# Clustered attention, mixture of experts and gated MLP on one core: mask copies, idle-time matmuls and expert 0's input moved

## The chip, the cores and the metric

The program runs on one core of a Trainium2 chip. The metric is device microseconds of one execution, and before the change it is 753.95 us (median of three runs, 753.9 to 755.81). TensorE (PE) multiplies and writes PSUM; VectorE (DVE) and ScalarE (ACT) read PSUM; GpSimd (POOL) works on SBUF; SyncE (SP) issues nearly all DMAs. Each engine runs its instructions in program order and waits on semaphores.

## The reference

Three stages follow each other (shapes in brackets).

```python
# attention: q, k, v [2, 8, 768, 64], 16 centroids per head
mask = argmax(q_n @ c_n)[:, :, :, None] == argmax(k_n @ c_n)[:, :, None, :]
scores = where(mask, q @ k.T / 8, -1e9)
attn = exp(scores - max) / (sum + 1e-9)
x = (attn @ v)                                   # -> [1536, 512]
# mixture of experts: each token to one of 8, at most 384 tokens each
e = argmax(x @ w_gate);  p = softmax(x @ w_gate)[e]
x = p * (relu(x @ w1[e]) @ w2[e])                # w1 [8, 512, 1024]
# gated MLP
out = (silu(x @ w_gate2) * (x @ w_val)) @ w_out  # 512 -> 1536 -> 512
```

## The kernel before

**Attention.** The 16 heads (2 batches of 8) are worked on as 8 pairs; an even and an odd head share a pair. A head has 6 query tiles of 128, so there are 96 tiles, and one loop (`run`, L504) goes over them. In the loop's step for tile g stand, in the order of `CFG['order']`: the exponentials of tile g+1 (`soft`, ACT, L378, out P), the sums of a finished group of three tiles (`evac`), the scores of tile g+2 (`qk`, four PE products, L365, out s, followed by a DVE maximum, L368, out nm), the transposes of tile g's P (`pt`, PE L397; one half copied by ACT, L400, the other by DVE, L402), then a list of extra steps for that tile (`bg[g]`: the first at B0, the others at B1), and every third tile the product with v (`pv`, L416, out acc). Score tiles have two PSUM buffers, so `qk` of tile g+2 waits until `soft` has read tile g.

**Preparation of a pair.** A pair's q and k are loaded (`load`, ldq, ldk), transposed by PE (`tr`, L169), split by ACT, DVE and POOL into a rounded part H and a rest L, and moved by DMAs (`moves`, L150) into the operands Aq, Ak, qB, kB. The cluster masks join the score product as 16 extra rows of qB and kB: `assign`, `pick`, `first` make a one-hot matrix, and `mask` writes its transpose to a tile oT (ACT) and moves it into qB and kB by four small DMAs. `CFG['offs']` and, for pair 1, `CFG['offs1']` say in which tile each step is issued, counted from the start of the pair before; pair 2's k is transposed first in tile 9 (offset -3 before tile 12). Pair 0 is prepared ahead of the loop: `mask0` (L277) writes the even head's rows straight into qB and kB, then copies all four row groups to oT (DVE the q rows, L305; ACT the k rows, L306) and moves the odd head's rows by two DMAs. The odd head of pair 0 starts at tile 6.

**SP's queue.** DMAs are issued in program order. With the code before, after pair 0's moves come: the two mask moves from oT, six small loads of the gate weights (`unit`, R and R2), the six q moves of pair 1, the loads of pair 2's q and k (four DMAs of 192 KB, issued in tile 0), the six k moves of pair 1 (192 KB each), and pair 1's four mask moves.

**The clock filler.** `warm` (L498) issues n transposes of the identity whose result nobody reads.

**Expert 0 during the last tiles.** Weight blocks of 128x1024 come through a pool of four buffers named raw (`load`, L947). Expert 0's eight blocks are split by quarters (`piece(i, k, eng)`, L972): half k of block i is rounded by ACT (eng 1) or POOL (eng 0), L982, and POOL takes the rest, L983. After the second half of a block the step named in L986 follows, such as the next load. `head` (L989) loads 128 token rows xa into a raw buffer; `slots` takes another raw buffer XA, into which `take_head` (L1007) writes their transpose split in two. Pieces run from the loop's extra steps (`spare`, L1541) and around `evac` (`pieces`, L1540). `tail` (L1066) finishes expert 0's first 128 tokens (`head1` by W1, `fold`, `head2` by W2) while the last tokens are scattered to their experts' rows. Experts and gated MLP follow and are untouched.

Of the kernel before, what the change touches and what calls it, by code (L numbers as in the profile page):

```python
# [10 lines left out]
F32 = mybir.dt.float32  # L11
F32R = mybir.dt.float32r
# [11 lines left out]
class Attention:  # L24
# [137 lines left out]
    def tr(self, n, nm, half):  # L162
# [10 lines left out]
        nc.scalar.activation(out=Ht[:, sl], in_=flat, func=AF.Copy, scale=s)  # L173
        if CFG["xe"]["qk".index(nm)] == "a":
            nc.scalar.activation(out=X[:, sl], in_=flat, func=AF.Copy, scale=s)  # L175
# [102 lines left out]
    def mask0(self):  # L278

        nc, st = self.nc, self.pairs[0]  # L280
        J, C, S = self.J, self.C, self.S
        HJ = J // 2
        st["oT"] = self.one.tile([4 * C, S], F32R, tag="oT", name="oT")
        ohv = st["oh"].rearrange("p j s c -> p j (s c)")
        ps = []
        for half in range(2):
            t = self.ps_m.tile([4 * C, HJ, 128], F32, tag="mm", name="otp")
            for jj in range(HJ):
                nc.tensor.transpose(t[:, jj, :], ohv[:, half * HJ + jj, :], self.ident)
            ps.append((slice(half * HJ * 128, (half + 1) * HJ * 128), t.rearrange("p j t -> p (j t)")))  # L290
        q, k = slice(0, 2 * C), slice(2 * C, 4 * C)

        def queries(sl, flat):
            nc.vector.tensor_copy(st["Bq"][64:64 + C, 0, sl], flat[0:C])

        def keys(sl, flat):
            nc.scalar.activation(out=st["Bk"][64:64 + C, 0, sl], in_=flat[2 * C:3 * C], func=AF.Identity,
                                 scale=self.sc[2 * C:3 * C, 0:1], bias=self.sc[2 * C:3 * C, 1:2])

        keys(*ps[0])  # L300
        queries(*ps[1])
        keys(*ps[1])
        queries(*ps[0])
        for sl, flat in ps:
            nc.vector.tensor_copy(st["oT"][q, sl], flat[q])  # L305
            nc.scalar.activation(out=st["oT"][k, sl], in_=flat[k], func=AF.Identity, scale=self.sc[k, 0:1],  # L306
                                 bias=self.sc[k, 1:2])
        for si, nm in enumerate("qk"):
            r0 = 2 * si * C
            self.move(st["B" + nm][64 - C:64, 1], st["oT"][r0 + C:r0 + 2 * C])  # L310

    def mask(self, n, half):
        nc, st = self.nc, self.pairs[n]
# [189 lines left out]
    def run(self, cent, gate, early, fill, after, spare, pieces, go):  # L503
# [5 lines left out]
        bg = {}  # L509
        for n in range(1, self.NP):  # L510
            s0 = 2 * J * (n - 1)
            st = self.prep_steps(n)
            for nm, o in CFG["offs" if n > 1 else "offs1"]:
                if n == 1 and nm in ("q0", "q1"):
                    continue
                bg.setdefault(s0 + o, []).append(st[nm])
            if n + 1 < self.NP:
                bg.setdefault(s0 + CFG["load"], []).append(lambda n=n: self.load(n + 1, "qk"))
            if n > 1:
                bg.setdefault(s0 + 5, []).append(lambda n=n: self.load(n, "v"))  # L520
        self.warm(self.ps_m, "mm", 13)
# [11 lines left out]
        a = [self.assign0(0), self.assign0(1)]  # L533
# [1 line left out]
            next(a[i])  # L535
        low = self.tr0(1, "q")
        self.warm(self.ps_m, "mm", 18)
        self.mask0()
        self.unit(gate)
        early()  # L540
        self.unit2()
        low()
        self.moves(1, 0, "q")
        self.moves(1, 1, "q")
        for e in range(self.E + 1):
            bg.setdefault(14 + 4 * e, []).append(lambda e=e: fill(e))
        for g, st in spare.items():
# [1 line left out]
        self.qk(0)  # L549
        self.soft(0)  # L550
        self.qk(1)

        chains, moves, ready = [], [], {}
        outs = {}
        for G in range(4 * self.NP - 1):
            n, half, r = self.group(G)
            if r == 1:
                outs[(G + 1) * HJ + CFG["oc"][half if n + 1 < self.NP else 2]] = n, half

        def trickle(g, tok):  # L560
            if chains and tok in CFG["mt" if g < NG - 2 * J else "mt2"] and g >= chains[0][0]:
                if next(chains[0][1]) is None:
                    moves.append(chains.pop(0)[1])
            if moves and tok == CFG["pt"] and g not in (s0 + 7, s0 + 8):
                if next(moves[0], 0) == 0:
                    moves.pop(0)

        for g in range(NG):
            G, c = divmod(g - HJ, HJ)
            steps = bg.pop(g, [])  # L570
            for tok in CFG["order"]:
# [12 lines left out]
                elif tok == "O" and g in outs:  # L584
                    n, half = outs[g]
# [22 lines left out]
        G, n = 2 * NH - 1, self.NP - 1  # L608
# [30 lines left out]
            pass  # L639


CFG = {'px': 'a', 'mt2': ['S', 'E', 'Q', 'T0'], 'mt': ['B1'], 'pt': 'V0', 'pe': 1, 'ms': [5, 2, 2], 'mr': 5, 'order': ['S', 'E', 'Q', 'T0', 'T1', 'B0', 'O', 'V0', 'B1'], 'offs': [['k0', -3], ['q0', -2], ['q1', -1], ['k1', 0], ['a', 1], ['t', 3], ['f', 6], ['m0', 7], ['m1', 8]], 'xe': 'da', 'me': 'a', 'ee': 'a', 'ec': 1, 'oc': [5, 5, 2], 'offs1': [['q0', 4], ['k0', 0], ['k1', 1], ['a', 2], ['t', 3], ['f', 5], ['m0', 6], ['m1', 7], ['q1', 0]], 'load': 0}


class Router:
# [250 lines left out]
class Experts:  # L896
# [79 lines left out]
    def piece(self, i, k, eng):  # L976

        nc = self.nc
        h, l = self.chunk(0, i)[1]()
        t = self.loads[0, i]  # L980
        ks = slice(2 * k, 2 * k + 2)
        (nc.scalar.copy if eng else nc.gpsimd.tensor_copy)(out=h[:, ks], in_=t[:, ks])  # L982
        nc.gpsimd.tensor_tensor(out=l[:, ks], in0=t[:, ks], in1=h[:, ks].bitcast(F32), op=ALU.subtract)  # L983
        if k == 1:
            del self.loads[0, i]
            (lambda: self.load(4), self.head, self.slots, lambda: self.load(5), lambda: self.load(6), lambda: None,  # L986
             lambda: None)[i]()

    def head(self):  # L989

        rt = self.rt
        t = self.raw.tile([128, 4, 256], F32, tag="raw", name="raw").rearrange("p a b -> p (a b)")[:, 0:self.DM]
        i = self.nc.sync.dma_start(out=t, in_=rt.rows[rt.first:])
        assert len(rt.puts) == rt.J
        rt.after(i, rt.puts)
        rt.reads.append(i)
        self.xa = t

    def slots(self):
        self.XA = self.raw.tile([128, 2, self.KD, 128], F32R, tag="raw", name="XA")  # L1000

    def turn_head(self, at):
        self.pa = at.ps_m.tile([128, self.KD, 128], F32, tag="mm", name="xa")
# [67 lines left out]
    def tail(self, at, go):  # L1071

        nc, rt, KD = self.nc, self.rt, self.KD
        self.room(at)
        a = self.fold(0)
        off = rt.offsets(self.keep[1], at.ps_t.tile([128, 3, 128], F32, tag="t", name="t")[:, 0, 0:self.E])
        next(a)
        yield
        self.rows(0, 0, 1, 2)
        nc.gpsimd.memset(rt.gap, 0.0)  # L1080
        next(a)
        next(a)
        go(4)
        for _ in range(6):
            next(off)
        next(a)
        for i in off:
            end = i
        go(12)
        a = self.fold(1)  # L1090
        rt.after(self.split(0, 7), [end])
        for _ in a:
            pass
        b = self.head2(at)
        for _ in range(16):
            next(b)
        self.cnt0, self.cnt1 = [self.count(1, e, None, rt.CP) for e in range(2)]
        for _ in range(8):
            next(b)
        self.px = [at.ps_s.tile([128, 2, 512], F32, tag="s", name="xp") for _ in range(2)]  # L1100
        for k in range(KD):
            self.turn(0, k)
        with self.tc.If(self.cnt0 > 128):
            for k in range(KD):
                self.turn(1, k)
            with self.tc.If(self.cnt0 > MERGED):
                for k in range(KD):
                    self.turn(2, k)
        for _ in b:
            pass  # L1110
# [392 lines left out]
def tile_clustered_attention_moe_swiglu(ctx, tc, q, k, v, cent, gate, w1, w2, wg, wv, wo, out, cap):  # L1503
    nc = tc.nc
    B, H, S, D = q.shape
    J = S // 128
    E, DM, F = w1.shape
    N = B * S
    const = ctx.enter_context(tc.tile_pool(name="const", bufs=1))
    raw = ctx.enter_context(tc.tile_pool(name="rawp", bufs=NRAW))  # L1510
    with tc.manual_schedule():
        ident = const.tile([128, 128], F32, name="ident")
        with ExitStack() as c2:
# [3 lines left out]
            with ExitStack() as c1:  # L1517
# [4 lines left out]
                ex = Experts(tc, rt, w1, w2, ident, raw, keep)  # L1522
# [7 lines left out]
                def first():  # L1530
# [5 lines left out]
                g0 = 2 * J * (at.NP - 2) + 9  # L1536
                at.free = g0 + 4
                P = lambda i, h, eng: lambda: ex.piece(i, h, eng)
                L = lambda i: lambda: ex.load(i)
                pieces = [P(1, 1, 1), P(2, 0, 1), P(3, 1, 1), P(4, 0, 1), P(5, 1, 1), P(6, 0, 1)]  # L1540
                spare = {g0: [first], g0 + 1: [L(1), P(0, 0, 0)], g0 + 2: [L(2), P(0, 1, 0)], g0 + 3: [L(3), P(1, 0, 0)],  # L1541
                         g0 + 5: [P(2, 1, 0)], g0 + 6: [P(3, 0, 0)], g0 + 8: [P(4, 1, 0)],
                          g0 + 9: [at.most, P(5, 0, 0), L(7)], g0 + 10: [lambda: None, lambda: ex.turn_head(at)],
                         g0 + 11: [ex.take_head, P(6, 1, 0)]}
                go = lambda n, it=ex.head1(at): [next(it) for _ in range(n)]
                front = at.run(cent, gate, rt.setup, rt.fill, after, spare, pieces, go)
                next(front)
# [42 lines left out]
```

## Time and profile before

| | |
|---|---|
| median of three runs | 753.95 us |
| the profiled execution | 752.9 us, its span 751.2 us |
| PE busy (matmuls / weight loads) | 97% / 81% of the span |
| DVE, ACT, POOL busy | 68%, 53%, 37% |
| attention | from 15 us to about 261 us |
| granted TensorE clock, mean | 0.997 |

A row of the timeline reads: start, duration, engine, line, operation, output<-inputs, shape, count, and in brackets the idle time before it and what ended that. Neighbouring instructions of one kind share a row.

### The profile page before, as it was taken

What the parts mean: (1) busy time and instruction counts of PE and PEld (TensorE: products, weight loads), DVE (VectorE), ACT (ScalarE), POOL (GpSimd) and SP (SyncE); (2) the same over time, 40 slices, a digit from 0 to 9 for tenths busy, and PEclk for the clock granted to TensorE, in tenths of its full rate; (3) what the DMA queues carried; (4) which work ended last, traced back from release to release, by engine and by line L of the source; (5) the groups of instructions that cost most, each with busy time, mean ns of one, the idle gap of its engine ahead of it and who ended that gap; (6) DMA issues with size and microseconds to landing.
All of it is one profiled execution on the core that took longest, in us unless ns stands there. A gap on an engine that the chain in (4) does not pass through costs nothing.

```text
span 751.2 us, 12723 instructions
## 1 busy us (share of the span) xinstructions
PE 731.3 (97%) x4310; PEld 608.7 (81%) x4310; DVE 509.4 (68%) x863; ACT 394.5 (53%) x763; POOL 280.3 (37%) x267
## 2 busy tenths in 40 slices
PE   7999999999999999999999999999999999999996
PEld 6777777767776789999999998788888888888885
DVE  4667777688787756666676567866766677676333
ACT  6777686877768754666667534542332222232110
POOL 6120211212125854555694334343333322333245
PEclk9999999999999999999999999999999999999999
DMA  9857869547256337688877733232122111210012
GB/s 203 176 137 205 203 181 250 129 108 173 48 157 205 101 125 241 220 253 267 264 248 239 217 116 106 89 89 80 57 67 74 57 57 56 85 29 0 1 57 112
DMA packets 103790, 102.92 MB, mean 137 GB/s; under 512 B 30896, under 2 KB 90800, under 8 KB 103696
## 3 DMA queue, kind: packets, MB, share of 16 engines
q1 hardware_dynamic: 101632, 95.37, 45.9%
q0 software_dynamic: 1920, 6.29, 2.2%
q8 instruction: 56, 0.92, 0.5%
q14 instruction: 38, 0.31, 0.1%
q10 hardware_dynamic: 144, 0.03, 0.0%
HBM read 68.48 MB, written 12.85 MB: 108 GB/s over the span
## 4 chain that ended last, share of the span: by engine, by line
PE 50%; DVE 4%; issue 3%; ACT 3%; POOL 1%; DMA 1%; DVEq 0%; ACTq 0%; POOLq 0%; SPq 0%
PE o L1456 12%; PE g L1438 12%; PE v L1438 12%; PE yp L1223 4%; PE hp L1223 3%; PE yp L1215 2%; PE hp L1215 2%; PE yp L1224 2%; PE hp L1224 1%; ACT W1h L967 1%; DVE gtmp L1415 1%; POOL out L1467 1%; DMA raw<-in_moe_w 1%; DVE gtmp L1414 0%; DVE hp L1237 0%
## 5 line engine op out<-in xcount | busy, mean ns | idle before, releaser
L368 DVE TENSOR_REDUCE nm<-s 128x1 f32<-128x768 f32 x96 | 91.1, 950 | 12.3 <-PE s L365 10.9
L968 POOL TENSOR_TENSOR W2l<-raw,W2h 128x1024 fp32r<-128x1024 f32 x29 | 69.1, 2396 | 66.8 <-ACT W2h L967 66.6
L378 ACT ACTIVATE P<-s,nm 128x768 f32<-128x768 f32 x96 | 86.6, 902 | 12.1 <-DVE nm L368 11.7
L397 PE MATMUL t<-ident,P 128*128 128x128 f32 x576 | 81.2, 275 | 0.9 <-ACT PT L400 0.7
L1445 POOL TENSOR_TENSOR ghl<-u,ghh 128x512 fp32r<-128x512 f32 x36 | 50.1, 1392 | 76.1 <-ACT ghh L1444 76.1
L397 PEld LDWEIGHTS t<-ident,P 128*128 128x128 f32 x576 | 68.9, 141 | 7.6 <-DVE PT L402 2.0
L416 PE MATMUL acc<-PT,ldv 128*64 128x384 f32 x384 | 69.2, 495 | 0.0
L1464 DVE TENSOR_TENSOR acc<-o,acc 128x512 f32<-128x512 f32 x60 | 41.5, 692 | 33.1 <-PE o L1456 32.9
L1223 PE MATMUL yp<-H,W2h 128*128 128x256 f32 (+3 forms) x224 | 61.7, 354 | 2.0 <-DVE H L1244 1.3
L365 PE MATMUL s<-Ak,Aq 128*128 128x384 f32 x192 | 58.8, 387 | 4.6 <-ACT P L378 3.8
L1223 PE MATMUL hp<-X,W1h 128*128 128x256 f32 (+3 forms) x224 | 61.0, 352 | 1.2 <-PE yp L1224 0.8
L1442 DVE TENSOR_TENSOR u<-sg,g 128x512 f32<-128x512 f32 x36 | 24.8, 688 | 54.8 <-ACT sg L1441 52.0
L400 ACT COPY PT<-t 128x384 f32<-128x384 f32 x96 | 45.7, 476 | 27.3 <-PE t L397 27.1
L1444 ACT CAST ghh<-u 128x512 fp32r<-128x512 f32 x36 | 22.4, 621 | 68.3 <-DVE u L1443 68.3
L1224 PE MATMUL yp<-H,W2l 128*128 128x128 f32 (+3 forms) x224 | 54.2, 242 | 0.0
L1224 PE MATMUL hp<-X,W1l 128*128 128x128 f32 (+3 forms) x224 | 54.0, 241 | 0.1
L402 DVE COPY PT<-t 128x384 f32<-128x384 f32 x96 | 52.4, 546 | 0.9 <-PE t L397 0.9
L968 DVE TENSOR_TENSOR W1l<-raw,W1h 128x1024 fp32r<-128x1024 f32 x28 | 43.3, 1565 | 13.8 <-ACT W1h L967 13.5
L365 PEld LDWEIGHTS s<-Ak,Aq 128*128 128x128 f32 x192 | 29.2, 190 | 28.6 <-ACT P L378 17.7
L365 PE MATMUL s<-kB,qB 80*128 80x384 f32 (+1 forms) x192 | 50.4, 343 | 0.3 <-issue 0.2
L416 PEld LDWEIGHTS acc<-PT,ldv 128*64 128x64 f32 x384 | 25.1, 136 | 28.0 <-issue 27.1
L176 POOL TENSOR_TENSOR Lk<-Xk,Hk 128x384 fp32r<-128x384 f32 x14 | 14.0, 1003 | 89.6 <-ACT Xk L175 89.6
(303 smaller groups left out, 1932.2 us busy)
## 6 DMA issues: line engine op xcount, KB each, us to landing
raw<-in_moe_w SPq DMA_DIRECT2D x64, 512.0 KB, 5.0
Ak<-Hk SPq DMA_DIRECT2D x32, 192.0 KB, 4.4
moe_rows<-zero SPq DMA_DIRECT2D x8, 768.0 KB, 5.3
raw<-in_moe_w_gate SPq DMA_DIRECT2D x12, 512.0 KB, 3.6
raw<-in_moe_w_val SPq DMA_DIRECT2D x12, 512.0 KB, 3.8
raw<-in_moe_w_out SPq DMA_DIRECT2D x12, 512.0 KB, 3.6
xr<-moe_rows SPq DMA_DIRECT2D x17, 256.0 KB, 4.1
ldq<-in_q SPq DMA_DIRECT2D x16, 192.0 KB, 4.1
```

The source lines that it names most:

```text
L365: nc.tensor.matmul(ps[:, c, 0:HS], lhsT=ql[:, qs], rhs=kr[:, c * HS:(c + 1) * HS], start=a == 0, stop=a == 1)
L368: nc.vector.tensor_reduce(out=nm, in_=ps[:, :, 0:HS], axis=AX.XY, op=ALU.max, negate=True)
L378: nc.scalar.activation(out=P, in_=ps[:, :, 0:HS], func=AF.Exp, bias=nm, accum_out=self.pairs[n]["sum"][:, i, r:r + 1])
L397: nc.tensor.transpose(ps[:, jj, :], P[:, a, jj * 128:(jj + 1) * 128], self.ident)
L402: nc.vector.tensor_copy(PT[:, js, cs], ps)
L416: nc.tensor.matmul(acc[c * D:(c + 1) * D], lhsT=v[:, c * HJ + j], rhs=PT[:, c * HJ + j, :], start=j == 0, stop=j == HJ - 1, tile_position= ...
L968: j = (nc.vector if e and i < 4 else nc.gpsimd).tensor_tensor(out=l, in0=t, in1=h.bitcast(F32), op=ALU.subtract)
L1223: self.nc.tensor.matmul(out[:, :, 0:w], lhsT=W[0][:, k, cols], rhs=mov[:, :, k, 0:w], start=k == 0, stop=False)
L1224: self.nc.tensor.matmul(out[:, 0, 0:w], lhsT=W[1][:, k, cols], rhs=mov[:, 0, k, 0:w], start=False, stop=k == ks - 1)
L1438: nc.tensor.matmul(ps[which], lhsT=W[a], rhs=self.Y[b][:, k, ts], start=k + i == 0, stop=k == KD - 1 and i == 2)
L1445: nc.gpsimd.tensor_tensor(out=hl[:, fc], in0=u, in1=hh[:, fc].bitcast(F32), op=ALU.subtract)
L1456: nc.tensor.matmul(p[t], lhsT=h[a][:, fc, t * 128:(t + 1) * 128], rhs=W[b][:, fc], start=fc == 0 and i == 0, stop=fc == 1 and i == 2)
```

## The change

`mask0` becomes a generator of three parts. The first (even head's rows) stays where it was; the copies of the first 384 columns to oT go to tile 0's step B0; the copies of the other 384 columns, the two mask moves, `unit` (the gate loads) and the q moves of pair 1 go to tile 1's step B0. The preparation of pair 1 from `k0` on moves back by one tile, and the loads of pair 2 from tile 0 to tile 2. Nine unread transposes stand after tile 1's scores. XA is taken in `head`, in place of a raw buffer, and the token rows land in its second half. The last quarter of block 6 that ACT rounded next to an `evac` moves to `tail`; POOL takes the other one.

```diff
@@ mask0
         queries(*ps[0])
+        yield
         for sl, flat in ps:
             nc.vector.tensor_copy(st["oT"][q, sl], flat[q])
             nc.scalar.activation(out=st["oT"][k, sl], in_=flat[k], ...)
+            if sl.start == 0:
+                yield
         for si, nm in enumerate("qk"):
             self.move(st["B" + nm][64 - C:64, 1], st["oT"][r0 + C:r0 + 2 * C])
+        yield
@@ run
-                bg.setdefault(s0 + CFG["load"], []).append(lambda n=n: self.load(n + 1, "qk"))
+                bg.setdefault(s0 + CFG["load"] + 2 * (n == 1), []).append(lambda n=n: self.load(n + 1, "qk"))
...
-        self.mask0()
-        self.unit(gate)
+        masks = self.mask0()
+        next(masks)
         early()
         self.unit2()
         low()
-        self.moves(1, 0, "q")
-        self.moves(1, 1, "q")
+
+        def rest():
+            next(masks)
+            self.unit(gate)
+            self.moves(1, 0, "q")
+            self.moves(1, 1, "q")
+
+        bg.setdefault(0, []).insert(0, lambda: next(masks))
+        bg.setdefault(1, []).insert(0, rest)
...
         self.qk(1)
+        self.warm(self.ps_t, "t", 9)
@@ CFG, offs1
-[['q0', 4], ['k0', 0], ['k1', 1], ['a', 2], ['t', 3], ['f', 5], ['m0', 6], ['m1', 7], ['q1', 0]]
+[['q0', 4], ['k0', 1], ['k1', 2], ['a', 3], ['t', 4], ['f', 6], ['m0', 7], ['m1', 8], ['q1', 0]]
@@ piece, head
-            (lambda: self.load(4), self.head, self.slots, lambda: self.load(5), ...)[i]()
+            (lambda: self.load(4), self.head, lambda: None, lambda: self.load(5), ...)[i]()
...
-        t = self.raw.tile([128, 4, 256], F32, tag="raw", name="raw").rearrange("p a b -> p (a b)")[:, 0:self.DM]
+        self.XA = self.raw.tile([128, 2, self.KD, 128], F32R, tag="raw", name="XA")
+        t = self.XA[:, 1].rearrange("p k t -> p (k t)").bitcast(F32)
@@ tail
         a = self.fold(1)
+        self.piece(6, 1, 1)
         rt.after(self.split(0, 7), [end])
@@ the kernel function
-                pieces = [..., P(5, 1, 1), P(6, 0, 1)]
+                pieces = [..., P(5, 1, 1)]
-                         g0 + 11: [ex.take_head, P(6, 1, 0)]}
+                         g0 + 11: [ex.take_head, P(6, 0, 0)]}
```

SP's queue before, from the last of pair 1's six q moves on (the gate loads stand ahead of those): pair 2's loads (ldq, ldk), pair 1's k moves, pair 1's mask moves.

```order
L150 DMA Aq<-Lq 64x768
L138 DMA ldq<-in_q 128x6x64 x2
L138 DMA ldk<-in_k 128x6x64 x2
L150 DMA Ak<-Hk 64x768 x2
L150 DMA kB_114<-Lk 64x768
L150 DMA Ak<-Hk 64x768 x2
L150 DMA kB_114<-Lk 64x768
L150 DMA qB_112<-oT 16x768 x2
L150 DMA kB_114<-oT 16x768 x2
```

The same stretch of SP's queue in the changed kernel.

```order
L150 DMA Aq<-Lq 64x768
L150 DMA Ak<-Hk 64x768 x2
L150 DMA kB_114<-Lk 64x768
L150 DMA Ak<-Hk 64x768 x2
L150 DMA kB_114<-Lk 64x768
L138 DMA ldq<-in_q 128x6x64 x2
L138 DMA ldk<-in_k 128x6x64 x2
L150 DMA qB_112<-oT 16x768 x2
L150 DMA kB_114<-oT 16x768 x2
```

Pair 2's four loads moved behind pair 1's six k moves; what stands ahead of the first row is the same in both, and so is what follows the last.

ACT at the loop's start before: the mask rows (kB, oT), then tiles 0 to 2 (P are exponentials, PT transposed halves, Hk and Xk pair 1's k).

```order
L297 ACTIVATE kB_113<-otp,sc 16x384 x2
L306 ACTIVATE oT<-otp,sc 32x384 x2
L378 ACTIVATE P,sum<-s,nm 128x768 x2
L400 COPY PT<-t 128x3x128
L173 ACTIVATE Hk<-trp 128x384
L175 ACTIVATE Xk<-trp 128x384
L378 ACTIVATE P,sum<-s,nm 128x768
L400 COPY PT<-t 128x3x128
```

The same in the changed kernel.

```order
L297 ACTIVATE kB_113<-otp,sc 16x384 x2
L382 ACTIVATE P,sum<-s,nm 128x768 x2
L404 COPY PT<-t 128x3x128
L307 ACTIVATE oT<-otp,sc 32x384
L382 ACTIVATE P,sum<-s,nm 128x768
L404 COPY PT<-t 128x3x128
L307 ACTIVATE oT<-otp,sc 32x384
L173 ACTIVATE Hk<-trp 128x384
L175 ACTIVATE Xk<-trp 128x384
```

The two oT copies moved from ahead of the first exponentials to behind the first PT copies of tiles 0 and 1, and pair 1's k behind them.

ACT in the last tiles before, with the roundings of expert 0's W2 (W2h) around `evac` (ol).

```order
L982 CAST W2h<-raw 128x2x256
L431 COPY ol<-acc 64x384
L982 CAST W2h<-raw 128x2x256
L400 COPY PT<-t 128x3x128
L378 ACTIVATE P,sum<-s,nm 128x768
```

The same in the changed kernel.

```order
L994 CAST W2h<-raw 128x2x256
L435 COPY ol<-acc 64x384
L404 COPY PT<-t 128x3x128
L382 ACTIVATE P,sum<-s,nm 128x768
L404 COPY PT<-t 128x3x128
```

The second rounding left this place; it now stands in `tail`, ahead of the rounding of the whole block 7.

## Rows read from the trace of the kernel before

**Rows 1.** The page, busy time of each engine over the span.
```profile
PE 731.3 (97%) x4310; PEld 608.7 (81%) x4310; DVE 509.4 (68%) x863; ACT 394.5 (53%) x763; POOL 280.3 (37%) x267
```
**Rows 2.** PE's waits, whole span then 44 to 240: us, times, longest.
```profile
PE s L365 <- ACT P L378: 3.8, 9, 1.4
...
PE s L365 <- ACT P L378: 2.0, 7, 0.3
```
**Rows 3.** Timeline at the loop's start, columns as told above.
```profile
15.28 1.01 DVE L305 CAST oT<-otp 32x384 fp32r<-32x384 f32 x2
...
15.87 1.22 ACT L306 ACTIVATE oT<-otp,sc 32x384 fp32r<-32x384 f32 x2 [0.38 <-DVE oT L305]
...
16.22 1.80 DVE L368 TENSOR_REDUCE nm<-s 128x1 f32<-128x768 f32 x2
...
17.19 0.90 ACT L378 ACTIVATE P<-s,nm 128x768 f32<-128x768 f32 x1
...
18.24 0.62 PE L365 MATMUL s<-Ak,Aq 128*128 128x384 f32 x2 [1.40 <-ACT P L378]
```
**Rows 4.** Stretches: length, busy of PE, PEld, DVE, ACT, POOL, clock, DMA, GB/s.
```profile
19.00:20.00 1.00, 1.00 (x7) 0.95 (x6) 0.69 (x1) 0.12 (x2) 0.00 (x0) 0.51 0.89 194
20.00:21.00 1.00, 1.00 (x7) 1.00 (x6) 0.68 (x2) 0.42 (x1) 0.00 (x0) 0.50 1.03 221
21.00:22.00 1.00, 1.00 (x5) 1.00 (x5) 0.14 (x1) 0.78 (x3) 0.00 (x0) 0.50 0.91 246
22.00:23.00 1.00, 1.00 (x8) 0.90 (x7) 0.43 (x1) 1.00 (x4) 0.83 (x1) 0.78 0.85 283
```
**Rows 5.** Timeline, transposes of tiles 0 and 2, ACT's PT copy of tile 1.
```profile
19.07 1.48 PE L397 MATMUL t<-ident,P 128*128 128x128 f32 x6
...
22.88 0.48 ACT L400 COPY PT<-t 128x384 f32<-128x384 f32 x1
...
24.05 0.82 PE L397 MATMUL t<-ident,P 128*128 128x128 f32 x6
```
**Rows 6.** Timeline of SP's DMA issues.
```profile
21.79 0.53 SPq L150 DMA_DIRECT2D kB<-oT  x1
22.42 0.68 SPq L117 DMA_DIRECT2D R<-in_moe_w_gate  x1
...
26.40 0.60 SPq L150 DMA_DIRECT2D Aq<-Hq  x1
...
32.97 1.29 SPq L138 DMA_DIRECT2D ldk<-in_k  x2
...
39.08 0.60 SPq L150 DMA_DIRECT2D kB<-Lk  x1
```
**Rows 7.** Stretches of 2 us, columns as in rows 4.
```profile
28.00:30.00 2.00, 2.00 (x14) 0.88 (x9) 1.10 (x3) 0.97 (x3) 0.79 (x1) 1.00 0.95 203
...
40.00:42.00 2.00, 1.59 (x13) 1.33 (x11) 1.30 (x3) 1.90 (x6) 0.00 (x0) 1.00 0.91 212
42.00:44.00 2.00, 2.00 (x16) 1.11 (x16) 1.07 (x2) 1.82 (x4) 0.42 (x1) 1.00 0.31 66
```
**Rows 8.** Timeline of PE, pair 2's k in tile 9.
```profile
42.10 0.49 PE L169 MATMUL trp<-ident,ldk 128*128 128x128 f32 x3
```
**Rows 9.** Timeline near the attention's end.
```profile
254.69 0.62 ACT L982 CAST W2h<-raw 128x512 fp32r<-128x512 f32 x1 [1.65 <-DMA raw<-in_moe_w]
...
255.86 0.88 PE L397 MATMUL t<-ident,P 128*128 128x128 f32 x6 [0.71 <-ACT PT L400]
```
**Rows 10.** Timeline, POOL and ACT pieces, and PE's products with W2.
```profile
259.32 1.28 POOL L983 TENSOR_TENSOR W2l<-raw,W2h 128x512 fp32r<-128x512 f32 x1
...
275.97 0.59 ACT L1053 COPY hA<-ha 128x512 f32<-128x512 f32 x1 [1.54 <-PE ha L1023]
...
275.93 2.40 POOL L968 TENSOR_TENSOR W2l<-raw,W2h 128x1024 fp32r<-128x1024 f32 x1
...
277.23 0.33 PE L1022 MATMUL ya<-HA,W2h 128*128 128x256 f32 x1
```

More of the change, by code (lines that the diff above doesn't have):

```diff
@@ L639, in run @@
             pass
-CFG = {'px': 'a', 'mt2': ['S', 'E', 'Q', 'T0'], 'mt': ['B1'], 'pt': 'V0', 'pe': 1, 'ms': [5, 2, 2], 'mr': 5, 'order': ['S', 'E', 'Q', 'T0', 'T1', 'B0', 'O', 'V0', 'B1'], 'offs': [['k0', -3], ['q0', -2], ['q1', -1], ['k1', 0], ['a', 1], ['t', 3], ['f', 6], ['m0', 7], ['m1', 8]], 'xe': 'da', 'me': 'a', 'ee': 'a', 'ec': 1, 'oc': [5, 5, 2], 'offs1': [['q0', 4], ['k0', 0], ['k1', 1], ['a', 2], ['t', 3], ['f', 5], ['m0', 6], ['m1', 7], ['q1', 0]], 'load': 0}
+CFG = {'px': 'a', 'mt2': ['S', 'E', 'Q', 'T0'], 'mt': ['B1'], 'pt': 'V0', 'pe': 1, 'ms': [5, 2, 2], 'mr': 5, 'order': ['S', 'E', 'Q', 'T0', 'T1', 'B0', 'O', 'V0', 'B1'], 'offs': [['k0', -3], ['q0', -2], ['q1', -1], ['k1', 0], ['a', 1], ['t', 3], ['f', 6], ['m0', 7], ['m1', 8]], 'xe': 'da', 'me': 'a', 'ee': 'a', 'ec': 1, 'oc': [5, 5, 2], 'offs1': [['q0', 4], ['k0', 1], ['k1', 2], ['a', 3], ['t', 4], ['f', 6], ['m0', 7], ['m1', 8], ['q1', 0]], 'load': 0}
 class Router:
@@ L985, in piece @@
             del self.loads[0, i]
-            (lambda: self.load(4), self.head, self.slots, lambda: self.load(5), lambda: self.load(6), lambda: None,
+            (lambda: self.load(4), self.head, lambda: None, lambda: self.load(5), lambda: self.load(6), lambda: None,
              lambda: None)[i]()
@@ L997, in head @@
         self.xa = t
-    def slots(self):
-        self.XA = self.raw.tile([128, 2, self.KD, 128], F32R, tag="raw", name="XA")
     def turn_head(self, at):
@@ L1539, in tile_clustered_attention_moe_swiglu @@
                 L = lambda i: lambda: ex.load(i)
-                pieces = [P(1, 1, 1), P(2, 0, 1), P(3, 1, 1), P(4, 0, 1), P(5, 1, 1), P(6, 0, 1)]
+                pieces = [P(1, 1, 1), P(2, 0, 1), P(3, 1, 1), P(4, 0, 1), P(5, 1, 1)]
                 spare = {g0: [first], g0 + 1: [L(1), P(0, 0, 0)], g0 + 2: [L(2), P(0, 1, 0)], g0 + 3: [L(3), P(1, 0, 0)],
```

## The prediction, made before the changed kernel ran

> **What bounds the kernel now.** I read the page's busy shares first, then the table of PE's waits, then the timeline and the stretches at the three places that the change touches. The page has PE busy for 97% of the span [rows 1], and the table of waits shows PE waiting for an exponential 7 times and 2.0 us in all over the 196 us from 44 to 240 [rows 2]. So from about 44 us on PE sets the pace of the attention: a microsecond that PE loses there is not made up, and one that another engine saves there gives nothing. The time can change only where PE waits or runs at half clock. Three such places lie in the change: the loop's start (15 to 24), pair 2's k in tile 9 (42), and the last tiles (254 to 277).
>
> At the start the oT copies stand on DVE (1.01 for two, from 15.28) and on ACT (1.22 for two, from 15.87), the first exponentials begin at 17.19, and the scores of tile 2 at 18.24 after the longest wait of the run, 1.40 us for the score buffer [rows 2, 3]. Then the granted clock is 0.51, 0.50, 0.50 and 0.78 of full in four stretches, 19 to 23: the lower level, 1.2 GHz, for some 3.4 us [rows 4]. Six transposes take 1.48 us there and 0.82 in tile 2 [rows 5]. Half clock for 3.4 us costs at most 1.7 us of PE work.
>
> **Part 1, oT copies off the start.** Removed ahead of the first exponentials are 1.01 us on DVE and 1.22 on ACT. This gives little there: after its oT copies ACT was done at 15.87+1.22 = 17.09 and began P at 17.19, and P also needs DVE's maximum, the first of two that share 1.80 us from 16.22, so 0.90 each and done at 17.12 [rows 3]. DVE's maximum began at 16.22 as the scores came, about when its copies were done (16.29). I take −0.1.
>
> **Part 2, nine unread transposes.** They stand in PE's order between tile 1's and tile 2's scores, in the gap of 1.40 us. From 0.82 for six they take 1.23 at full clock [rows 3, 5], so they are hidden if they start at once. If the clock is granted at full through 19 to 23 because PE does not idle first, PE gains up to 1.7 us; if not, nothing, and at half clock the nine would be 2.2 us by the 1.48 row, of which 0.8 would show. Bounds −1.7 and +0.8; the fall stands directly behind the 1.40 us of idleness, so I take −1.4.
>
> **Part 3, oT copies in tiles 0 and 1.** ACT now has 2 × 0.61 = 1.22 us more between tile 0's PT copy and pair 1's k. In the four stretches it is busy 0.12, 0.42, 0.78 and 1.00, so idle 1.68 in all, but most of it early and 0.00 in the last [rows 4]. With the clock repaired PE brings its work sooner, which takes idle time away. Each copy of ACT also follows a DVE half on the same PSUM tile. So the copies cost between 0 (all in the idle time) and +1.4 (their own 1.22 and a handover, such as the 0.38 before ACT's oT row in [rows 3]). I take +1.3. The start nets 0 by tile 2, with bounds −1.8 and +1.2.
>
> **Part 4, what stands behind the oT moves on SP.** SP works in order. The move kB<-oT was issued at 21.79, then the six gate loads from 22.42, and pair 1's first q move at 26.40; those loads alone hold SP for 3.98 us [rows 6]. Now the second oT copy on ACT comes behind tile 1's PT copy. In before that PT copy ended at 22.88+0.48 = 23.36 [rows 5]. Pair 1's Hk and Xk, two copies of the same 128x384 shape and so 0.96, no longer stand ahead of it and the first oT copy, 0.61, does: 23.0. The second oT copy follows with 0.61 and 0.1 for the handover, and ends at 23.7. The move is issued at 23.75, 1.95 later, and the gate loads keep their 3.98, so pair 1's q moves start at 28.35.
>
> What follows is where the price arises. In before the 16 transfers of 192 KB (6 q moves, 4 loads, 6 k moves) were issued from 26.40 to 39.68. In the seven stretches of 2 us from 28 to 42 the DMA engines carry 203 in the first and 212 in the last, with shares of 0.95 and 0.91: they are saturated, and only 66 GB/s are left from 42 on [rows 7]. 16 × 196.6 KB = 3146 KB, which over 26.40 to about 42.0 is 202 GB/s, so the queue drains at 42.0 to 42.6. Pair 2's k was then the tenth of 16 (ldk issued at 32.97), and PE found it landed when it transposed it at 42.10, without idle time before [rows 6, 8]. Now pair 2's loads stand last of the 16. The same 15.6 us from 28.35 on end at 44.0, and k has landed at about 44.1 (43.9 to 44.5). PE asks for it at 42.1 plus what the start nets. With 0 it waits 2.0 us; if the start gains, the wait takes the gain back, because the load's landing and not PE's pace decides. So by the transposes of tile 9 PE is at 44.1 instead of 42.10: **+2.0**, bounds 0 (loads stay ahead of PE) and +2.4. Pair 1's mask moves, behind the 16, also come 2 us later; pair 1's even head is read only from tile 12 on, three tiles after the wait, and that cover I take as enough, at nothing.
>
> **Part 5, expert 0 in the last tiles.** ACT's second rounding of block 6 stood idle 1.65 us for its weights at 254.69 and ended at 255.31; PE then waited 0.71 us for the PT copy behind it [rows 9]. That rounding is gone from there. What is late next is the P of the tile, or nothing, so I take −0.7. XA's new place, the second half of its own buffer, frees `head` from nothing that PE waited for, and I count it at nothing. Bounds −0.9 (a little more if ACT's next instructions come earlier too) and 0.
>
> In `tail` the rounding is 0.62 [rows 9], and ACT idles 1.54 before the copy at 275.97, which holds it [rows 10]. POOL gets a subtraction of 1.28 (the like row at 259.32) ahead of block 7's, which starts at 275.93 and lasts 2.40 [rows 10]. POOL then starts block 7's at about 277.2, while PE reads W2h of the last blocks from 277.23. The first piece's rest is needed by then, with next to nothing to spare. I take +0.05, bounds 0 and +0.3, and by adding up −0.65 for part 5.
>
> **Sum.** Start 0, k load +2.0, tail −0.65: +1.35. On the profiled execution, 752.9 us (span 751.2 and 1.7 around it), that is 754.25. The median of the runs is 1.05 above the profiled execution, so on it the sum gives 753.95 + 1.35 = 755.3.
>
> A rule weighed against this sum: PE's waits show an engine with next to no slack [rows 2]. The Trainium skill (Perfetto Trace Analysis, Identifying the Most-Contended Engine) calls matmul busy time a bad measure and wants the weight loads' busy share. By that share, 81% instead of 97% [rows 1], PE would have a fifth of its time left and would take the 2.0 us back later. Against it stand the few waits of rows 2, but it is a rival below.
>
> **Rivals.**
>
> *A, the wait brings the clock down.* A PE wait of 2 us in tile 9 resembles that of 1.40 us which preceded the fall at 19 [rows 3, 4]. If the clock again runs at the lower level for some 3.4 us, PE loses up to 1.7 more; I take +1.4. The time is 755.3 + 1.4 = 756.7, slower than before. It decides from a wait as long as that at 18.24. Against it: in the stretches around 42 PE is busy 1.59 and 2.00 of 2 us, at a clock of 1.00 [rows 7], so the wait stands more alone.
>
> *B, the load is in time.* If oT's copies go out at their old time (ACT's idle time takes them), the 16 transfers run as before and end at 42.1, or the DMA orders k ahead. Then only the tail is left, 753.95 − 0.65 = 753.3, with a start at 0.
>
> *C, the start is a gain.* The repaired clock gives −1.8 in all, ACT's 1.68 us of idle time takes the copies, and the load is in time: 753.95 − 1.8 − 0.7 = 751.45. For it speaks that ACT's first stretch is busy for 0.12 only; against it that the idle time comes ahead of PT's copy, while the copies stand behind it.
>
> *D, the loss is made up.* PE has slack by weight loads; the wait of 2.0 comes and goes: 753.3. Rows 2 speak against it: with waits of 2.0 us in 196, nothing else holds PE back that could be overtaken.
>
> **How the numbers follow.** My forecast 755.3 has 0.36, A 0.25, B 0.17, C 0.15, D 0.07. A difference below 0.3%, 2.26 us, can't be told from no change by a measurement of this kernel, so the bounds are 751.69 and 756.21. C is faster (0.15, less a little for a tail gain that falls short, 0.14). Slower is A and the upper end of the forecast, whose load wait could be 2.4 and whose tail could gain nothing or lose a little: 0.25 + 0.08 = 0.33. The rest, 0.53, is the same. The likeliest case's own range is 754.2 to 756.4; the range of 751.7 to 757.1 leaves out the better half of C and the top of A.
>
> **What the changed profile would show.** Granted clock near 1.00 in 19 to 23 if part 2 holds; below it, the transposes were too late or too few. ACT's second oT copy ends near 23.7 and kB<-oT is issued near 23.75, the first q move of pair 1 near 28.35; if these come by 22 and 26.5, part 4 falls. The transposes of pair 2's k (trp from ldk) start near 44.1 with idle time of about 2 us, ended by a DMA; without it, B or C. The clock behind it separates A. In 44 to 240 PE's waits stay near 2.0 us in all; if they shrink by as much as was lost, D. Near 255 no ACT rounding waits for weights, and PE's 0.71 is gone; POOL's block 7 begins near 277.2 and the products with W2 do not wait for it over 0.3 us. What would make the forecast wrong most of all is a k load that lands by 42.

## The result, and the profile after

The changed kernel takes 759.56 us (median of ten, 756.33 to 762.94), the kernel before 754.25 (ten, 752.71 to 756.91): ratio 1.0058, 95% interval 1.0039 to 1.0077, so by the ratio about 4.4 us slower (the two medians lie 5.3 apart). Two later sets of twelve gave 1.0055 [1.0033, 1.0077] and 1.0061 [1.0038, 1.0083]. The predicted 755.3 was too low, and the time lies above the range.

The profiled execution took 762.94 us. Busy shares on its page, which answer to [rows 1], look as before:

```profile
PE 738.3 (97%) x4319; PEld 615.7 (81%) x4319; DVE 510.3 (67%) x863; ACT 394.7 (52%) x763; POOL 280.5 (37%) x267
```

First, how to line the two traces up. Up to the first scores PE runs the same instructions in both kernels, yet this execution is 4.26 us late there. The timeline of PE before, six transposes and the second half of tile 0's scores:

```profile
6.85 0.85 PE L193 MATMUL s<-ident,ldk 128*128 128x128 f32 x6 [0.48 <-DMA ldk<-in_k]
...
15.54 0.59 PE L365 MATMUL s<-kB,qB 80*128 80x384 f32 x2
```

The same two places after, and the start of the loop behind them:

```profile
6.84 1.51 PE L193 MATMUL s<-ident,ldk 128*128 128x128 f32 x6 [0.22 <-DMA ldk<-in_k]
...
19.80 0.68 PE L369 MATMUL s<-kB,qB 80*128 80x384 f32 x2 [0.76 <-DVE qB L294]
21.02 1.15 PE L505 MATMUL warm<-ident 128*128 128x128 f32 x9
22.55 0.62 PE L369 MATMUL s<-Ak,Aq 128*128 128x384 f32 x2 [0.38 <-ACT P L382]
...
26.19 0.55 PE L169 MATMUL trp<-ident,ldk 128*128 128x128 f32 x3 [0.60 <-ACT oT L307]
27.21 0.62 PE L369 MATMUL s<-Ak,Aq 128*128 128x384 f32 x2 [0.47 <-ACT P L382]
...
30.19 0.62 PE L369 MATMUL s<-Ak,Aq 128*128 128x384 f32 x2 [1.02 <-ACT P L382]
```

The six transposes take 1.51 instead of 0.85, about as long as the 1.48 at a granted 0.50 in [rows 4, 5]: by these durations PE ran at the lower clock level through this prologue (this trace's stretches before 17 show 1.00 all the same, so here only the durations tell). Over all profiles below the prologue is 0 to 4.3 us late with no relation to the kernel, so I compare from the scores at 15.54 on. In place of the one wait of 1.40 [rows 3] the changed start has four, 2.47 together. Its clock did not fall: the stretches 22 to 24 and 24 to 26 are granted 1.00.

SP's issues after, answering to [rows 6]:

```profile
28.25 0.53 SPq L150 DMA_DIRECT2D kB<-oT  x1
28.87 0.68 SPq L117 DMA_DIRECT2D R<-in_moe_w_gate  x1
...
32.85 0.59 SPq L150 DMA_DIRECT2D Aq<-Hq  x1
...
44.41 2.44 SPq L138 DMA_DIRECT2D ldk<-in_k  x2
```

And PE at pair 2's k, answering to [rows 8], with the stretches around it:

```profile
46.52 0.82 PE L401 MATMUL t<-ident,P 128*128 128x128 f32 x6
50.12 0.55 PE L169 MATMUL trp<-ident,ldk 128*128 128x128 f32 x3 [2.79 <-DMA ldk<-in_k]
```

```profile
46.00:48.00 2.00, 1.33 (x10) 1.06 (x9) 1.51 (x3) 1.95 (x5) 0.00 (x0) 1.00 0.76 161
48.00:50.00 2.00, 0.00 (x0) 0.00 (x0) 0.14 (x1) 0.10 (x1) 0.00 (x0) 1.00 0.75 159
50.00:52.00 2.00, 1.88 (x11) 1.03 (x13) 0.00 (x0) 1.29 (x3) 0.34 (x1) 0.89 0.14 25
52.00:54.00 2.00, 2.00 (x7) 0.52 (x4) 0.00 (x0) 0.57 (x3) 0.65 (x1) 0.50 0.00 0
54.00:56.00 2.00, 2.00 (x14) 1.96 (x14) 1.26 (x2) 0.74 (x2) 0.00 (x0) 0.75 0.01 4
```

PE stands still for 2.79 us until k lands, and then works at the lower level (1.2 GHz) for some 3 us. Near the end PE's wait of [rows 9] is gone:

```profile
264.62 0.82 PE L401 MATMUL t<-ident,P 128*128 128x128 f32 x6
```

This table follows one instruction through all kernels: its start there less its start before, at five places of before's timeline (scores at 15.54, scores at 40.63 which are the last before tile 9's wait, tile 10's transposes at 45.42, scores at 252.39, transposes at 255.86). A step from one column to the next is time lost or won between them.

| kernel | 15.54 | 40.63 | 45.42 | 252.39 | 255.86 | ratio [95%] |
|---|---|---|---|---|---|---|
| changed, first profile | 4.26 | 5.08 | 9.67 | 9.63 | 8.76 | 1.0058 [1.0039, 1.0077] |
| c1_after | 2.67 | 3.49 | 6.23 | 6.20 | 5.33 | 1.0055 [1.0033, 1.0077] |
| c2_after | 0.92 | 1.74 | 5.96 | 5.87 | 5.01 | 1.0061 [1.0038, 1.0083] |
| e1_load0 | 0.20 | 0.92 | 1.06 | 1.06 | 0.19 | 0.9986 [0.9963, 1.0009] |
| e2_before_load2 | 0.97 | 1.20 | 1.98 | 1.95 | 1.97 | 1.0002 [0.9986, 1.0018] |
| e7_gate3 | 0.25 | 0.96 | 1.24 | 1.06 | 0.19 | 1.0010 [0.9988, 1.0032] |
| e11_load1 | 0.86 | 1.57 | 1.80 | 1.77 | 0.89 | 0.9989 [0.9963, 1.0015] |
| e6_fill | −0.06 | 0.67 | 3.69 | 5.94 | 5.07 | 1.0080 [1.0053, 1.0108] |
| e9_fill24 | 0.26 | 0.97 | 4.10 | 5.42 | 4.56 | 1.0063 [1.0036, 1.0090] |
| e8_load0_nowarm | 4.33 | 5.14 | 5.27 | 5.19 | 4.33 | 1.0015 [0.9986, 1.0044] |
| e10_start | 0.52 | 1.24 | 1.38 | 1.28 | 1.42 | 0.9999 [0.9976, 1.0022] |
| e3_tail | 0.59 | 1.85 | 1.85 | 1.73 | 0.87 | 0.9982 [0.9962, 1.0001] |
| e4_warm9 | 0.24 | 0.05 | 0.05 | 0.02 | −0.06 | 0.9982 [0.9962, 1.0003] |
| e5_tail_warm9 | 0.72 | −0.24 | −0.24 | −0.30 | −1.16 | 0.9963 [0.9935, 0.9992] |

Less the prologue, the first profile loses 0.82 at the start and 4.59 around tile 9, keeps that to 252, and wins 0.87 in the last tiles: +4.50, against +4.4 by the ratio. Behind 255.86 it ends 10.0 late, for its clock fell once more, from 396.3 on, among the experts, which the change doesn't touch; e11's fell at 325.5 and e9's at 392.0. So the ends of single profiles can't be compared.

### The profile page after: what moved, and what is told of

The parts are those of the page before. It is cut to its first block, busy times and chain, and to the rows that moved or that the text cites. A ratio compares the mean times of both kernels' runs of the same rounds, so it can differ in the third digit from the quotient of the medians.

```text
span 761.2 us, 12742 instructions
## 1 busy us (share of the span) xinstructions
PE 738.3 (97%) x4319; PEld 615.7 (81%) x4319; DVE 510.3 (67%) x863; ACT 394.7 (52%) x763; POOL 280.5 (37%) x267
## 4 chain that ended last, share of the span: by engine, by line
PE 50%; DVE 4%; ACT 3%; issue 2%; POOL 1%; DMA 1%; DVEq 0%; ACTq 0%; POOLq 0%; SPq 0%
PE o L1467 12%; PE g L1449 11%; PE v L1449 11%; PE yp L1234 4%; PE hp L1234 3%; PE hp L1226 2%; PE yp L1226 2%; PE yp L1235 2%; PE hp L1235 1%; DVE gtmp L1426 1%; ACT W1h L979 1%; POOL out L1478 1%; DMA raw<-in_moe_w 1%; ACT W2h L979 1%; DVE hp L1248 0%
```

## The experiments

**Is the wait for pair 2's k the loss?** In the changed kernel, the loads go back to tile 0, ahead of pair 0's oT moves:

```diff
-bg.setdefault(s0 + CFG["load"] + 2 * (n == 1), [])...
+bg.setdefault(s0 + CFG["load"], [])...
```

> The changed kernel with pair 2's q and k loads back in tile 0; everything else as changed. Theory W (the wait for pair 2's k, 2.79 us, and the fall of the clock behind it, about 1.6 us, are the loss): the loads are issued ahead of pair 0's oT moves, k lands before 40, the transposes of tile 9 don't wait for a DMA, the clock stays at 1.00 from there to tile 20, and the time falls by 4.4 us against the changed kernel, to 754 to 756, ratio to the kernel before 0.998 to 1.003. Rival P (the loss is the clock of the prologue, where six transposes took 1.51 us in the profiled run after and 0.85 before, about 4.3 us): the time stays at about 759, ratio 1.004 to 1.008, whatever the wait does. Rival S (the oT copies between the first exponentials are the loss): between, about 758.

Measured 753.89 (before 754.91 beside it). The timeline of PE has no wait at pair 2's k:

```profile
43.01 0.49 PE L169 MATMUL trp<-ident,ldk 128*128 128x128 f32 x3
```

The loss is gone with one edit that moves four DMAs. S, the oT copies, is out as the cause of the whole, for they stay. P, the prologue's clock, is out as the cause of the difference, though this one profile also has a fast prologue; c1 and c2 settle it below.

**Which part makes k late: its place in the queue or the queue's later start?** Four cases: the changed kernel and three new ones. First the kernel before with the loads in tile 2, behind pair 1's k moves:

```diff
-bg.setdefault(s0 + CFG["load"], [])...
+bg.setdefault(s0 + CFG["load"] + 2 * (n == 1), [])...
```

> The kernel before with one edit: pair 2's q and k loads in tile 2 instead of tile 0, so that they stand behind pair 1's six k moves; pair 1's q moves still start at about 26.4. Theory W: k lands as the last of the sixteen transfers at 42.5 to 44, PE asks at 42.1, so a wait of 0.4 to 1.9 us, and if it is over about 1 us the clock falls behind it: +0.5 to +3.5 us, ratio 1.001 to 1.005. Theory P: no change, ratio 0.999 to 1.001.

```profile
44.02 0.55 PE L169 MATMUL trp<-ident,ldk 128*128 128x128 f32 x3 [0.56 <-DMA ldk<-in_k]
```

A wait of 0.56 and no fall behind it: by the trace, the place alone costs about half a microsecond. The time can't tell that from nothing (755.46 against 754.91, ratio 1.0002). Then the changed kernel with the gate loads behind everything:

```diff
             next(masks)
-            self.unit(gate)
...
+        bg.setdefault(3, []).append(lambda: self.unit(gate))
```

> The changed kernel with the six gate loads issued in tile 3, behind pair 2's loads, instead of in tile 1 ahead of pair 1's q moves. Pair 2's loads stay the last of the sixteen. If the wait comes from where the queue stands (3.98 us of issues ahead of the sixteen), pair 1's q moves start 4 us earlier, k lands about 1 us before PE asks, no wait and no fall: -4.4 us against the changed kernel, ratio to before 0.998 to 1.001. Rival: the place behind the k moves alone is the cause, then a wait of over 1 us stays and the ratio is 1.002 to 1.006.

Its timeline of PE, and SP's issues:

```profile
43.05 0.49 PE L169 MATMUL trp<-ident,ldk 128*128 128x128 f32 x3
```

```profile
24.73 0.58 SPq L150 DMA_DIRECT2D Aq<-Hq  x1
...
36.17 1.30 SPq L138 DMA_DIRECT2D ldk<-in_k  x2
```

The loads are still last of the sixteen; the queue starts right behind the oT moves, at 24.73 and so earlier than before, and k is in time (754.08 against 754.26). At last the changed kernel with the loads in tile 1, so that they stand between q and k moves as before while the queue starts late:

```diff
-...CFG["load"] + 2 * (n == 1)...
+...CFG["load"] + (n == 1)...
```

> The changed kernel with pair 2's loads in tile 1, so that among the sixteen transfers they stand between pair 1's q and k moves, as before, while the queue still starts some 2 us late. If the place among the sixteen is what makes k late: k lands about 4 us before PE asks, no wait in tile 9, pair 1's k moves land about 4 us later than in the changed kernel, still before tile 12, or with a wait of under 0.5 us at tile 10's or 12's scores; ratio to before 0.998 to 1.002. If the late start of the queue alone is the cause, a wait of over 1 us stays, for k or for pair 1's operands, and the ratio is 1.003 to 1.006.

```profile
43.66 0.49 PE L169 MATMUL trp<-ident,ldk 128*128 128x128 f32 x3
```

No wait (754.91 against 755.03). But k landed at 42.7, 1.0 ahead of PE and not the expected 4; before, it landed at 38.0, 4.1 ahead. So the later start uses up slack too, and neither alone makes the loss: the place makes a wait of 0.56, the later start none, both together one of 2.4 to 2.8 and what follows.

**The changed kernel again.**

> The changed kernel once more, beside three edits of it, for a second profile. Theory W: pair 2's k makes PE wait 2.5 to 3 us in tile 9 and the clock falls behind it again; ratio to the kernel before 1.004 to 1.008. Theory P (the late clock of the prologue, 4.3 us in the first profile, belongs to the change): the six transposes ahead of the first scores take 1.5 us again. If that is chance, 0.85 in this profile or in others of the same prologue.

> The changed kernel a third time, for whether the clock falls behind the wait in tile 9 (it did in the first profile, not in the second). If the fall is the rule, this profile shows 0.50 for 3 us behind it; if not, it is 1.00. Ratio to before 1.004 to 1.008 in either case, a wait of 2.5 to 2.8 us.

Pair 2's k and the stretches behind it in c1:

```profile
48.28 0.55 PE L169 MATMUL trp<-ident,ldk 128*128 128x128 f32 x3 [2.54 <-DMA ldk<-in_k]
```

```profile
48.00:50.00 2.00, 1.72 (x11) 0.94 (x13) 0.00 (x0) 1.13 (x3) 0.18 (x1) 1.00 0.18 35
50.00:52.00 2.00, 2.00 (x14) 1.27 (x11) 0.47 (x1) 1.10 (x3) 0.82 (x1) 1.00 0.00 0
```

And in c2:

```profile
46.38 0.55 PE L169 MATMUL trp<-ident,ldk 128*128 128x128 f32 x3 [2.39 <-DMA ldk<-in_k]
```

```profile
46.00:48.00 2.00, 1.62 (x9) 0.86 (x11) 0.00 (x0) 1.03 (x3) 0.08 (x1) 0.90 0.20 38
48.00:50.00 2.00, 2.00 (x8) 0.49 (x4) 0.00 (x0) 0.72 (x2) 0.92 (x1) 0.50 0.00 0
```

The wait is there each time (in c2 a little under the expected 2.5), the fall in two profiles of three. Neither follows the prologue, which was 2.67 late in the one without a fall and 0.92 in c2; c1's six transposes took 0.84 and not 1.5. Why waits of nearly the same length bring the clock down in one profile and not in another stays open. The price of the fall is read behind the wait: from k's transposes to tile 10's it is 4.97 us in the first profile and 5.00 in c2, against 3.32 before (42.10 to 45.42) and 3.37 in c1. That makes 1.65 and 1.68.

**Does keeping PE busy keep the clock?** Unread transposes ahead of pair 2's k, 20 in one tile:

```diff
+            if n == 2:
+                k0 = st["k0"]
+                st["k0"] = lambda: (self.warm(self.ps_m, "mm", 20), k0())
```

> The changed kernel with 20 more unread transposes (2.74 us at full clock) ahead of pair 2's k in tile 9, so that PE works while it waits. If idleness brings the clock down: k is transposed at the same time as in the changed kernel, the clock stays at 1.00 behind it, and the time falls by about 1.6 us, ratio to before 1.002 to 1.005. Rival: the clock falls anyway, then the ratio stays at 1.004 to 1.008. Rival: without idleness the DMA wait itself is unchanged but the fillers end later than k lands: the gain is 0.5 to 1 us less.

and 24 in two tiles (12 and 12):

> The changed kernel with 24 unread transposes in two tiles of 12 ahead of pair 2's k, so that the pool's two PSUM buffers stay in the same turn as in the changed kernel (one tile of 20 exchanged them for all that follows, and that kernel lost another 1.5 us in later tiles). If that exchange was the loss there, and idleness costs a fall in most executions: the wait for k is as long, no fall in the profile, ratio to before 1.002 to 1.005, at least 1 us under the changed kernel. If the fall is rare: the same as the changed kernel, 1.004 to 1.007.

PE in the second:

```profile
43.06 2.78 PE L505 MATMUL warm<-ident 128*128 128x128 f32 x24
46.17 0.52 PE L169 MATMUL trp<-ident,ldk 128*128 128x128 f32 x3 [0.33 <-PE warm L505]
```

Neither profile has a fall there (nor has c1, without fillers), but neither kernel is faster: 1.0080 and 1.0063, 759.33 and 758.77 against 754.26 and 754.67. The expected 1.6 us did not come back. The table shows where it went: 2.25 and 1.32 us lost between 45 and 252. Of the 2.25, 1.50 goes in two stops of PE at the first scores of a pair that need its mask rows (0.65 at 80.2, with no releaser in the profile, and 0.75 at 173.6, ended by the mask move kB<-oT); the second kernel has no such stops. The rest of the first and all of the second goes near 250, where ACT's rounding of W1h waits for its weights (0.88 us in the first); ACT's timeline of the second:

```profile
250.08 0.62 ACT L997 CAST W1h<-raw 128x512 fp32r<-128x512 f32 x1 [1.49 <-DMA raw<-in_moe_w]
```

That is a stall like that of [rows 9] in another tile. The exchange of PSUM buffers, which I blamed after the first, is not its cause, since the second has none; whether it made the two stops of the first is not shown. Why the weights come late just there stays open, and so the price of idleness is not shown by these two.

**The start alone**, with the loads in tile 0 and the last tiles as before:

```diff
-        self.mask0()
+        masks = self.mask0()
+        next(masks)
...
+        self.warm(self.ps_t, "t", 9)
```

> The change's start alone (mask copies in tiles 0 and 1, queue, nine transposes, pair 1's steps one tile later), with pair 2's loads in tile 0 and the last tiles as before. From the first experiment less the last part's gain: tile 8's scores +0.7 to +0.9 us later than before by the prologue's own time, PE's 0.71 us wait near 255 there again, ratio 1.000 to 1.002. Rival: the clock that is kept at the start is worth more than the waits for the oT copies: 0.998 to 1.000.

Measured 753.70 against 754.67: +0.72 at 40.63 less the prologue, and PE's wait near 255 is there again (0.85). The nine transposes were also left out of the first experiment's kernel (its `warm` line removed):

> The changed kernel with pair 2's loads in tile 0 (the first experiment) and without the nine unread transposes. If the nine hold the clock at the start: the granted clock is 0.50 for 3 to 4 us between 19 and 24, tile 8's scores come 0.5 to 1.5 us later than in the first experiment, ratio to before 0.999 to 1.001, against 0.9986 with them. Rival: the waits for the oT copies (0.47, 0.60, 1.02 us of PE) hide the lower clock: the same time as the first experiment.

PE's longest wait at the start and the stretches around it:

```profile
22.61 0.62 PE L369 MATMUL s<-Ak,Aq 128*128 128x384 f32 x2 [1.36 <-ACT P L382]
```

```profile
22.00:24.00 2.00, 1.39 (x10) 1.35 (x11) 0.77 (x2) 1.49 (x5) 0.00 (x0) 1.00 0.56 171
24.00:26.00 2.00, 1.65 (x13) 1.31 (x11) 2.00 (x4) 0.90 (x2) 0.00 (x0) 1.00 0.91 208
```

A wait of 1.36 without a fall, and the same 0.81 lost at the start: in this one profile the changed start keeps its clock without the nine. The ratio is 1.0015 against 0.9986 with them, and the intervals overlap, so the times decide nothing; the mean clocks below say more. In the kernel before, the nine alone:

> The kernel before with the nine unread transposes behind tile 1's scores and nothing else. If PE's 1.40 us of idleness ahead of tile 2's scores brings the clock down, the stretches 19 to 23 stay at 1.00, six transposes of tile 0 take 0.82 instead of 1.48, and -1.4 us (-1.8 to -0.5) result, ratio 0.9976 to 0.9995. Rival: the clock falls all the same, for the wait stays in part, or the gain is taken back by a later wait for ACT or the k load: 0, ratio 0.9995 to 1.0005.

```profile
16.00:17.00 1.00, 1.00 (x5) 0.99 (x5) 1.00 (x3) 0.67 (x2) 0.92 (x1) 0.74 0.82 277
17.00:18.00 1.00, 1.00 (x5) 0.90 (x5) 0.97 (x2) 0.89 (x2) 0.00 (x0) 0.50 1.00 212
```

In this profile the clock fell at 16, before the nine began at 17.41; they gained 0.19 from 15.54 to 40.63. 752.51 against 754.91, ratio 0.9982 with an interval that reaches past 1.

**The last tiles alone.**

> The kernel before with the change's last part alone: XA taken in head, the token rows in its second half, the quarters of block 6 moved. Expected: no rounding that waits for its weights near 254.7, PE's 0.71 us wait there gone, POOL's rest of block 7 about 1.3 us later with no wait of PE over 0.3: -0.7 us (-1.0 to 0), ratio 0.9985 to 1.000. A rival that POOL's later start delays the products with W2 gives +0.3 to +0.9, ratio 1.0005 to 1.001.

753.68 against 754.91. From 252.39 to 255.86 it wins 0.86, as all kernels with this part do (0.86 to 0.88), while e10 without it loses 0.14. **Both of these together**, the kernel before with the last part and the nine:

> The kernel before with the change's last part (XA in head, quarters of block 6) and the nine unread transposes, without the moved mask copies, queue and loads. The two alone gave 0.9982 each. If both hold and add: ratio 0.996 to 0.998, the fastest of all. If they share the same gain or were chance: 0.998 to 1.000.

751.68 against 754.67, ratio 0.9963 [0.9935, 0.9992]: the lowest ratio, what the two (0.9982 each) make together, and the only one whose interval stays under 1. Its clock did not fall at the start:

```profile
18.00:20.00 2.00, 1.45 (x10) 1.18 (x9) 0.98 (x2) 1.89 (x5) 0.00 (x0) 1.00 1.01 213
20.00:22.00 2.00, 2.00 (x17) 1.96 (x16) 1.46 (x3) 1.31 (x5) 0.00 (x0) 1.00 0.82 186
```

**How long was the clock low in the timed runs?** Each timed run has its mean granted clock on record, to three digits. Averaged over the runs of like kernels, with the standard error of the average:

| kernels | runs | the nine | wait for pair 2's k | mean clock |
|---|---|---|---|---|
| before, beside the experiments | 122 | no | none | 0.9947 ± 0.0002 |
| e2, e3 | 24 | no | 0.56 in e2 | 0.9948 ± 0.0004 |
| e4, e5 | 24 | yes | none | 0.9975 ± 0.0004 |
| e8 (changed start) | 12 | no | none | 0.9952 ± 0.0008 |
| e1, e7, e10, e11 (changed start) | 48 | yes | none | 0.9976 ± 0.0002 |
| changed, all three sets | 34 | yes | 2.4 to 2.8 | 0.9956 ± 0.0003 |
| e6, e9 (fillers over the wait) | 24 | yes | filled | 0.9966 ± 0.0004 |

The mean doesn't tell where in a run the clock was low. But with the nine it is higher by 0.0028 in the kernel before and by 0.0024 in the changed start, 2.1 and 1.8 us of clock in 755. So they do hold the clock in most runs, and e8's profile without a fall is not the rule. The changed kernel lies 0.0020 below the kernels that share its start and have k in time, 1.5 us of clock; the fall in its first profile, half clock for some 3.4 us, takes 1.7. By that, an estimate, the fall behind the wait comes in most of the timed runs too.

## Why the prediction was wrong

**The step that failed is part 4, "By the transposes of tile 9 PE is at 44.1": +2.0, and after it the choice of the case without a fall of the clock.** The mechanism was right. Taking 4.26 off for the prologue, kB<-oT was issued at 23.99 (predicted 23.75) and the first q move at 28.59 (28.35). But from there to k's landing I took 15.6 us, and it was 50.12 − 32.85 = 17.27 (17.02 in c1, 16.87 in c2, 17.09 in e2 with the loads last). The 15.6 ran to the end of the busy stretches at 42 and not to a landing, though [rows 7] still had 66 GB/s behind it. Before, the fifteenth of the sixteen landed at 42.2 and the mask move behind them at 43.0, so they took some 15.8 to 16.6 already there (an estimate, for the sixteenth's own landing is not on record). Part of the rest is a hole: the final stretches move 161 and 159 GB/s, but not because loads are slow. By single microseconds:

```profile
46.00:47.00 1.00, 1.00 (x9) 0.96 (x9) 0.52 (x2) 0.95 (x3) 0.00 (x0) 1.00 1.01 215
47.00:48.00 1.00, 0.33 (x4) 0.09 (x1) 1.00 (x2) 1.00 (x3) 0.00 (x0) 1.00 0.50 107
48.00:49.00 1.00, 0.00 (x0) 0.00 (x0) 0.14 (x1) 0.10 (x1) 0.00 (x0) 1.00 0.97 216
```

Where the DMA engines are busy (1.01, 0.97) the loads move 215 and 216; for half of the microsecond between, the engines stand idle. That hole follows SP's issue of the two k loads, which took 2.44 us and not 1.29 as in [rows 6]; why it took longer stays open, and so does what makes up the rest of the 17 (e7's two k loads were issued in 1.30, and k still landed 17.0 behind the first q move). So k came at 45.86 and not at 44.1: +3.76 against the 42.10 of before where I had +2.0. PE asked at 43.07, and the wait was 2.79.

**The clock.** I gave the fall (rival A) 0.25 and priced it at 1.4. It came in two of three profiles, by the mean clocks in most of the timed runs, and cost 1.65 where it came. A was the truer forecast in kind, and also too low: 755.3 + 1.4 lacks the longer wait.

**The start** nets +0.82 in all three profiles, where I took 0 with bounds −1.8 and +1.2. (My parts 1 to 3 add up to −0.2 and not 0, their upper bounds to 2.1 and not 1.2; and 1.22 with a handover of 0.38 is 1.60, not 1.4.) The clock held, as forecast. In e5, which keeps the copies at their old place and adds the nine, the start wins 0.96, less than the 1.4 of part 2; so the copies, and what moved with them, cost about 1.8, more than my 1.3. ACT's timeline of the changed kernel shows why:

```profile
25.47 0.67 ACT L307 ACTIVATE oT<-otp,sc 32x384 fp32r<-32x384 f32 x1 [1.10 <-DVE oT L306]
```

I had counted the copy's time and a handover of 0.38. ACT stood idle for 1.10 us until DVE's half was done, and the next exponential came that much later. As I had said of a gain, k's landing would have taken this loss in: it is part of the 3.76, for PE would have waited anyway.

**The last tiles** were forecast at −0.65 in sum and gave −0.87, the wait of 0.71 and a little more, as bounded; POOL's block 7 began at 277.2 of before's time (285.93 less the 8.76 of the table), as forecast.

**Rivals B, C and D** fall. k was not in time, the start was no gain, and what was lost by tile 10 was not made up: c1 is 6.23 late at 45.42 and 6.20 at 252.39. The Trainium skill (Perfetto Trace Analysis, Identifying the Most-Contended Engine) judges headroom by MFU, the share of peak arithmetic, and by the weight loads' busy share. That share is no sign of slack here: 81% went with none.

Summed with what was measured in the first profile: 0.82 at the start, 2.94 more until k, 1.65 for the fall, −0.87 at the end: 4.5. Without the fall it is 2.7 (c1). The measured +4.4 agrees with a fall in most runs; no trace of the timed runs shows where their clock was low.

## What to carry to other kernels

Where a load is moved behind others in a queue, work out its landing from the whole chain: what now releases the queue, what is issued ahead, and count to a landing, not to the end of the busy stretches. Two shifts that made PE wait 0.56 and nothing apart made it wait 2.4 to 2.8 together, with a fall of the clock on top in two profiles, because they used up the same slack. One profile can show a clock that most runs don't have; the mean clocks of all runs are the check. And a copy that is moved to an engine's idle time must be priced with the wait for its partner on the other engine.

## What the runs showed that I had not expected

The prologue of one and the same instruction stream ran at either clock level: six transposes took 0.85 or 1.51, and the first scores came up to 4.3 us apart between executions of all kernels. A single profile of two kernels can differ by that alone. A wait of 2.4 to 2.8 us brought the clock down in two profiles and left it in one. A stretch of 160 GB/s at the end of a queue was no slow transfer, but 215 with a hole in it.
